# The first two of seven products summed in a PSUM bank that ScalarE fills, in a fused attention and expert kernel

## The chip, the core and the metric

The kernel runs on one core of a Trainium2 chip. TensorE multiplies matrices into PSUM, VectorE (DVE), ScalarE (ACT) and GpSimd (POOL) work on tiles of 128 partitions, and SyncE (SP) issues transfers; ScalarE issues some as well. Each engine runs its own instructions in order and waits on semaphores for the others. The metric is device time in microseconds (us): the median of the runs, here 843.47 us over three runs (843.33 to 843.47).

## The reference

What is computed is a decaying linear attention over 4 x 8 heads of 768 steps, and two expert layers on its 3072 tokens:

```python
for t in range(S):
    state = gamma[None, :, None, None] * state + np.einsum('bhd,bhe->bhde', k[:, :, t], v[:, :, t])
    y[:, :, t] = scale * np.einsum('bhd,bhde->bhe', q[:, :, t], state)
...
a = x @ w1                      # 512 -> 1024
b = x @ w2
h = a * b @ w3                  # 1024 -> 1024
x = h @ w_out                   # 1024 -> 512
...
h = np.maximum(np.maximum(x @ w1, x @ w2), x @ w3)   # 512 -> 768
return (h @ w_out).astype(np.float32)                # 768 -> 512
```

All data are float32. In the kernel every operand is split into a high and a low part of a faster float type, and a product is three matmuls: high by high, high by low, low by high.

## The kernel before, in words

The work goes in stages, with the times of the profiled execution: attention (0 to 88 us), stage B (x @ w1 and x @ w2 and their product, 88 to 320), the merging of w3 with w_out (320 to 363), its application (363 to 494), stage H (the three projections and their maximum, 494 to 752), and the output stage (752 to the end).

Stages B, H and the output stage use a scheme of seven products on a two-by-two partition of the matrices. A block (`blk`, or `n` in the output stage) is 512 columns of each half of the tokens; it goes through products `q` = 0 to 6, and each product through its parts: 4 in B (`GA`), 3 in H (`GH`), 2 in the output stage (`r`). A part is 6 matmuls of 128x512 in B and H, 9 in the output stage. The parts of a product go to one of two sets of PSUM banks, "a" or "b", which change roles from block to block. `ORDER` (L44) says which set a product uses and whether it starts afresh: product 0 starts set a; product 1 starts set b; product 2 goes on adding to a; product 3 starts b again; 4 and 6 add to a, and 5 to b.

Products are combined by evictions. In B, ScalarE copies product 0 to the tile U (L496), VectorE adds product 1 to U (L498), ScalarE copies products 2 and 3 to C and E (L500, L502), VectorE finishes E and C (L504, L506), GpSimd multiplies C by U (L507), VectorE multiplies E by the last bank (L510). H is alike (L729 to L744), with a maximum over parts: for product 1 VectorE does an add for part 0, and an add and a maximum for each of parts 1 and 2. The output stage (L787 to L803) copies product 0 to y11 and VectorE adds product 1.

Operands are made two products ahead: `op_split` (L244) lets ScalarE cast the high part (L241) and VectorE subtract the low part (L242), into one of four slots `op`. Some are differences that `op_pre` (L252) computes on VectorE, called three products ahead (`d == 3`, L472): for product 2 two instructions on 128x1024 (L255, L256, the second into the tile T), for product 3 one (L259), for product 5 one (L261).

Beside this the weights of the next stage are decoded from 64-bit numbers. `step` alternates two halves: `decode_a` (VectorE L134 for the previous piece, L140, L142 for this one) and `decode_b` (ScalarE L149, which needs L142). `decode_front` (ScalarE L117, then GpSimd L119) prepares the next piece; new pieces are fetched by transfers on ScalarE's queue (L86). The class `Spread` (L179) hands these jobs out evenly over `tick` calls, one after each part. In the first group of stage B (`g == 0`, blocks 0 to 2) the list begins with seven idle jobs (L449), over 60 ticks.

The program order of each engine is the order in which this code is written; nothing reorders it later.

## Time and profile before

| what | us |
|---|---|
| median of three runs | 843.47 |
| the profiled execution's own time | 843.5 |
| its span, first to last instruction | 841.7 |
| TensorE matmuls busy (x4720) | 830.0 (99%) |
| VectorE busy (x725) | 589.0 (70%) |
| ScalarE busy (x560) | 365.5 (43%) |
| GpSimd busy (x121) | 120.8 (14%) |
| TensorE idle for VectorE or transfers, attention left out | 2.5 in 4 waits |

The granted TensorE clock is 1.00 of full speed in every stage. Busy time of matmuls overlaps, since each is shown from its start to its modelled end: a matmul is shown 0.39 us long, though the next starts sooner. The views used are the page, the waits by engine, the timelines of each engine (instructions in order of time), and the groups by line.

### The profile page before, as it was taken

To read this page: it belongs to the slowest core of one execution; us is meant where nothing else is said; L and a number is where in the kernel's file an instruction comes from. 1 tells how busy PE (TensorE), PEld (TensorE's weight loads), DVE (VectorE), ACT (ScalarE), POOL (GpSimd) and SP (SyncE) were. 2 spreads that over 40 slices of the span, in tenths; PEclk is the share of its full clock that TensorE was granted. 3 is DMA by queue.
4 is the path that set the end of the run, shared out by engine and by line. 5 is a ranking of instruction groups with operands and counts; after the bars stand their busy time and mean duration, and the time that the engine had idled before them with its cause. 6 is when DMAs were issued, how large, how long until landed. Compare 5 with 4: busy or idle time off the path is not lost.

```text
span 841.7 us, 12200 instructions
## 1 busy us (share of the span) xinstructions
PE 830.0 (99%) x4720; PEld 694.1 (82%) x4720; DVE 589.0 (70%) x725; ACT 365.5 (43%) x560; POOL 120.8 (14%) x121
## 2 busy tenths in 40 slices
PE   8999999999999999999999999999999999999998
PEld 8889888878888888888888888887888888888886
DVE  3898978898475756753574657678657665878793
ACT  2544455354434343633555453343333334335542
POOL 3444031302031322100201000200000010000000
PEclk9999999999999999999999999999999999999999
DMA  9998367759988967462495699829998899856522
GB/s 347 408 406 337 152 283 289 288 213 369 362 324 312 340 228 263 150 218 87 147 336 213 218 410 412 334 88 382 409 361 300 318 367 357 291 239 228 209 101 75
DMA packets 54634, 235.00 MB, mean 279 GB/s; under 512 B 6320, under 2 KB 6448, under 8 KB 39344
## 3 DMA queue, kind: packets, MB, share of 16 engines
q1 hardware_dynamic: 37728, 133.46, 40.8%
q10 hardware_dynamic: 16848, 100.76, 32.5%
q8 instruction: 37, 0.61, 0.3%
q14 instruction: 21, 0.17, 0.1%
HBM read 161.85 MB, written 72.35 MB: 278 GB/s over the span
## 4 chain that ended last, share of the span: by engine, by line
PE 74%; DVE 3%; DMA 2%; issue 1%; ACT 0%; ACTq 0%; DVEq 0%
PE bank L724 9%; PE bank L725 9%; PE bank L726 9%; PE bank L492 5%; PE bank L601 5%; PE bank L603 5%; PE bank L493 5%; PE bank L602 5%; PE bank L491 5%; PE bank L783 3%; PE bank L784 3%; PE bank L782 3%; PE bank L540 2%; PE bank L542 2%; PE bank L541 2%; DMA opsp<-op 1%
## 5 line engine op out<-in xcount | busy, mean ns | idle before, releaser
L724 PE MATMUL bank<-op,w 128*128 128x512 f32 x360 | 140.1, 389 | 0.3 <-DMA op<-opsp 0.3
L725 PE MATMUL bank<-op,w 128*128 128x512 f32 x360 | 140.2, 389 | 0.2 <-DVE op L242 0.2
L726 PE MATMUL bank<-op,w 128*128 128x512 f32 x360 | 140.1, 389 | 0.0
L491 PE MATMUL bank<-op,w 128*128 128x512 f32 x336 | 130.9, 390 | 1.0 <-DVE E L510 1.0
L492 PE MATMUL bank<-op,w 128*128 128x512 f32 x336 | 130.9, 390 | 1.0 <-DVE op L242 1.0
L493 PE MATMUL bank<-op,w 128*128 128x512 f32 x336 | 130.7, 389 | 0.0
L119 POOL TENSOR_SCALAR dec<-dec 128x512 f32<-128x512 f32 x64 | 47.5, 742 | 481.6 <-ACT dec L117 457.2
L724 PEld LDWEIGHTS bank<-op,w 128*128 128x128 f32 x360 | 67.6, 188 | 14.8 <-issue 0.7
L725 PEld LDWEIGHTS bank<-op,w 128*128 128x128 f32 x360 | 67.6, 188 | 14.5 <-DVE op L242 0.6
L726 PEld LDWEIGHTS bank<-op,w 128*128 128x128 f32 x360 | 67.6, 188 | 14.1
L491 PEld LDWEIGHTS bank<-op,w 128*128 128x128 f32 x336 | 63.1, 188 | 14.7 <-ACT U L496 1.4
L492 PEld LDWEIGHTS bank<-op,w 128*128 128x128 f32 x336 | 63.1, 188 | 14.4 <-DVE op L242 1.7
L602 PE MATMUL bank<-op,w 128*128 128x512 f32 x192 | 74.7, 389 | 0.0
L601 PE MATMUL bank<-op,w 128*128 128x512 f32 x192 | 74.7, 389 | 0.0
L603 PE MATMUL bank<-op,w 128*128 128x512 f32 x192 | 74.7, 389 | 0.0
L493 PEld LDWEIGHTS bank<-op,w 128*128 128x128 f32 x336 | 63.1, 188 | 13.1
L149 ACT ACTIVATE dec<-stg 128x512 int32<-128x512 uint32 x59 | 39.6, 672 | 69.6 <-DVE stg L142 64.6
L117 ACT ACTIVATE dec<-stg 128x512 f32<-128x512 f32 x59 | 39.1, 663 | 30.3 <-DMA stg<-in_wo_dram 17.4
L140 DVE TENSOR_SCALAR dec<-dec 128x512 int32<-128x512 int32 x64 | 34.1, 533 | 23.0 <-POOL dec L119 23.0
L142 DVE SCALAR_TENSOR_TENSOR stg<-stg,dec 128x512 int32<-128x512 int32 x59 | 42.5, 720 | 5.2 <-ACT E L502 0.4
L507 POOL TENSOR_TENSOR C<-C,U 128x512 f32<-128x512 f32 x24 | 36.1, 1526 | 54.3 <-DVE C L506 54.2
L602 PEld LDWEIGHTS bank<-op,w 128*128 128x128 f32 x192 | 36.0, 188 | 7.5
(177 smaller groups left out, 1494.0 us busy)
## 6 DMA issues: line engine op xcount, KB each, us to landing
op<-opsp ACTq DMA_DIRECT2D x77, 1024.0 KB, 7.5
opsp<-op SPq DMA_DIRECT2D x25, 1024.0 KB, 5.0
ck<-in_ck_dram SPq DMA_DIRECT2D x48, 512.0 KB, 10.2
opsp<-w SPq DMA_DIRECT2D x14, 1024.0 KB, 5.9
stg<-in_w3t_dram ACTq DMA_DIRECT2D x16, 512.0 KB, 3.4
hsp<-m SPq DMA_DIRECT2D x32, 256.0 KB, 6.6
stg<-in_w_dram SPq DMA_DIRECT2D x15, 512.0 KB, 10.7
stg<-in_w_dram ACTq DMA_DIRECT2D x14, 512.0 KB, 5.1
```

The costliest lines, as they stand in the source:

```text
L119: nc.gpsimd.tensor_scalar(out=df, in0=df, scalar1=MAX_HI, scalar2=MIN_HI, op0=ALU.min, op1=ALU.max)
L142: nc.vector.scalar_tensor_tensor(out=top, in0=top, scalar=-0x40000000, in1=dec, op0=ALU.bitwise_and, op1=ALU.bitwise_or)
L149: nc.scalar.activation(out=dec, in_=low.bitcast(U32), func=ACT.Copy, scale=2.0 ** -29)
L491: nc.tensor.matmul(ps, wh, x[:, 0, k, :], start=first and k == 0, stop=False, skip_group_check=True)
L492: nc.tensor.matmul(ps, wh, x[:, 1, k, :], start=False, stop=False, skip_group_check=True)
L493: nc.tensor.matmul(ps, wl, x[:, 0, k, :], start=False, stop=k == 1, skip_group_check=True)
L601: nc.tensor.matmul(ps, wh, x[:, 0, k, :], start=kk == 0 and k == 0, stop=False)
L602: nc.tensor.matmul(ps, wh, x[:, 1, k, :], start=False, stop=False)
L603: nc.tensor.matmul(ps, wl, x[:, 0, k, :], start=False, stop=kk == 3 and k == 1)
L724: nc.tensor.matmul(ps, wh, x[:, 0, k, :], start=first and k == 0, stop=False, skip_group_check=True)
L725: nc.tensor.matmul(ps, wh, x[:, 1, k, :], start=False, stop=False, skip_group_check=True)
L726: nc.tensor.matmul(ps, wl, x[:, 0, k, :], start=False, stop=k == 1, skip_group_check=True)
```

## The change

Three things change.

First, in B (from block 1 on), in H and in the output stage, ScalarE copies product 0 not to an SBUF tile but to the bank of set b in which product 1 of the same part is about to be computed. Product 1 no longer starts that bank afresh but adds to what was copied (`seeded`; in the output stage `q != 1`). The bank then holds the sum, and ScalarE copies it out: to U in B, to m11 for part 0 in H, to y11 in the output stage. VectorE's add is gone. For parts 1 and 2 of H, VectorE takes the maximum with the bank directly, one instruction instead of two. Block 0 of B works as before.

Second, in the first group of B the two differences for product 2 of the next block are issued at product 5, behind the split of the next block's product 0, and not at product 6.

Third, the list of decode jobs in that group has four idle jobs in front instead of seven.

```diff
--- before.py
+++ after.py
@@ -446,7 +446,7 @@
             if g == 0:
                 wq += [lambda i=i, u=u: fetch_w12(i, u) for i in range(GA, KF) for u in range(2)]
                 more(3)
-                side = Spread([idle] * 7 + [step] * (4 * GA), 2 * 28 + 4)
+                side = Spread([idle] * 4 + [step] * (4 * GA), 2 * 28 + 4)
             else:
                 x_st.close()
                 m_st, m_pl = stage_pool("m")
@@ -469,11 +469,13 @@
                             t = s + d
                             if t < 7 * NB:
                                 qd = quad_b(t // 7)
-                                if d == 3:
+                                if d == 3 and t % 7 != 2:
                                     op_pre(t // 7, t % 7, qd, quiet=True)
-                                else:
+                                elif d == 2:
                                     op_split(t, op_src(t // 7, t % 7, qd))
                                     store(opsp[t // 7, t % 7], op_t[t % 4].bitcast(F32))
+                                    if q == 5:
+                                        op_pre(n + 1, 2, quad_b(n + 1), quiet=True)
                         if s < 2:
                             store(opsp[0, s], op_t[s].bitcast(F32))
                         for job in late_w.pop(s, ()):
@@ -484,15 +486,18 @@
                     which, first = ORDER[q]
                     x = op_slot(s)
                     w = wslot(q).rearrange("p h (i k n) -> p h i k n", i=GA, k=2)
+                    seeded = blk > 0 and q == 1
                     for p in range(GA):
                         ps = sets[which][p]
                         for k in range(2):
                             wh, wl = w[:, 0, p, k, :], w[:, 1, p, k, :]
-                            nc.tensor.matmul(ps, wh, x[:, 0, k, :], start=first and k == 0, stop=False, skip_group_check=True)
+                            nc.tensor.matmul(ps, wh, x[:, 0, k, :], start=first and k == 0 and not seeded, stop=False, skip_group_check=True)
                             nc.tensor.matmul(ps, wh, x[:, 1, k, :], start=False, stop=False, skip_group_check=True)
                             nc.tensor.matmul(ps, wl, x[:, 0, k, :], start=False, stop=k == 1, skip_group_check=True)
                         u, c, e = (part(nm, p) for nm in "UCE")
                         if q == 0:
+                            nc.scalar.copy(out=sets["b"][p] if blk else u, in_=ps)
+                        elif seeded:
                             nc.scalar.copy(out=u, in_=ps)
                         elif q == 1:
                             nc.vector.tensor_tensor(out=u, in0=u, in1=ps, op=ALU.add)
@@ -717,27 +722,29 @@
                     which, first = ORDER[q]
                     x = quads4(gen_t[s - held] if held <= s < held + len(gen_t) else op_t[s % 4])
                     w = wslot(q, 256 * GH).rearrange("p h (i k n) -> p h i k n", i=GH, k=2)
+                    seeded = q == 1
                     for p in range(GH):
                         ps = sets[which][p]
                         for k in range(2):
                             wh, wl = w[:, 0, p, k, :], w[:, 1, p, k, :]
-                            nc.tensor.matmul(ps, wh, x[:, 0, k, :], start=first and k == 0, stop=False, skip_group_check=True)
+                            nc.tensor.matmul(ps, wh, x[:, 0, k, :], start=first and k == 0 and not seeded, stop=False, skip_group_check=True)
                             nc.tensor.matmul(ps, wh, x[:, 1, k, :], start=False, stop=False, skip_group_check=True)
                             nc.tensor.matmul(ps, wl, x[:, 0, k, :], start=False, stop=k == 1, skip_group_check=True)
                         u, c, e = (part(nm, p) for nm in "UCE")
                         if q == 0:
-                            nc.scalar.copy(out=u, in_=ps)
+                            nc.scalar.copy(out=sets["b"][p], in_=ps)
                         elif q == 2:
                             nc.scalar.copy(out=c, in_=ps)
                         elif q == 3:
                             nc.scalar.copy(out=e, in_=ps)
-                        elif q == 6:
+                        elif q in (1, 6):
+                            m = m12 if q == 6 else m11
                             if p:
-                                nc.vector.tensor_tensor(out=m12, in0=m12, in1=ps, op=ALU.max)
+                                nc.vector.tensor_tensor(out=m, in0=m, in1=ps, op=ALU.max)
                             else:
-                                nc.scalar.copy(out=m12, in_=ps)
+                                nc.scalar.copy(out=m, in_=ps)
                         else:
-                            m, v, (x0, x1), op = {1: (m11, u, (u, ps), ALU.add), 4: (m22, e, (ps, e), ALU.subtract),
+                            m, v, (x0, x1), op = {4: (m22, e, (ps, e), ALU.subtract),
                                                   5: (m21, c, (c, ps), ALU.subtract)}[q]
                             nc.vector.tensor_tensor(out=v if p else m, in0=x0, in1=x1, op=op)
                             if p:
@@ -779,14 +786,14 @@
                 ps = o_sets[n % 2][which][r]
                 o = slice(r * P, (r + 1) * P)
                 for k in range(3):
-                    nc.tensor.matmul(ps, wh[:, k, o], xh[:, k], start=first and k == 0, stop=False, skip_group_check=True)
+                    nc.tensor.matmul(ps, wh[:, k, o], xh[:, k], start=first and k == 0 and q != 1, stop=False, skip_group_check=True)
                     nc.tensor.matmul(ps, wh[:, k, o], xl[:, k], start=False, stop=False, skip_group_check=True)
                     nc.tensor.matmul(ps, wl[:, k, o], xh[:, k], start=False, stop=k == 2, skip_group_check=True)
                 y11, y12, y21, y22 = y_t[4 * r:4 * r + 4]
                 if q == 0:
+                    nc.scalar.copy(out=o_sets[n % 2]["b"][r], in_=ps)
+                elif q == 1:
                     nc.scalar.copy(out=y11, in_=ps)
-                elif q == 1:
-                    nc.vector.tensor_tensor(out=y11, in0=y11, in1=ps, op=ALU.add)
                     store(outv[r, 0, :, cols], y11, 0)
                 elif q == 2:
                     nc.scalar.copy(out=y21, in_=ps)
```

How the instructions now stand is told by their order, here at three places. Numbers at the end of a tile's name tell copies of a tile apart: bank_1094 to bank_1097 are set a of block 1 in B, and bank_1090 to bank_1093 its set b. Line numbers from L447 on differ between the two kernels.

ScalarE in stage B, around product 0 of block 1, before:

```order
L117 ACTIVATE dec_63<-stg_62 128x512
L241 CAST op_1103<-xr_94 128x1024
L149 ACTIVATE dec_63<-stg_62 128x512
L117 ACTIVATE dec_64<-stg_60 128x512
L241 CAST op_73<-xr_94 128x1024
L149 ACTIVATE dec_64<-stg_60 128x512
L117 ACTIVATE dec_63<-stg_61 128x512
L86 DMA stg_62<-in_w_dram 128x512
L241 CAST op_1101<-T 128x1024
L496 COPY U<-bank_1094 128x512
L496 COPY U<-bank_1095 128x512
L496 COPY U<-bank_1096 128x512
```

And with the change:

```order
L241 CAST op_1103<-xr_94 128x1024
L149 ACTIVATE dec_64<-stg_60 128x512
L117 ACTIVATE dec_63<-stg_61 128x512
L86 DMA stg_62<-in_w_dram 128x512
L241 CAST op_73<-xr_94 128x1024
L149 ACTIVATE dec_63<-stg_61 128x512
L117 ACTIVATE dec_64<-stg_62 128x512
L86 DMA stg_60<-in_w_dram 128x512
L241 CAST op_1101<-T 128x1024
L499 COPY bank_1090<-bank_1094 128x512
L499 COPY bank_1091<-bank_1095 128x512
L499 COPY bank_1092<-bank_1096 128x512
```

The last L149 and L117 ahead of the cast of T now belong to the next piece of weights (stg_61 and stg_62, where it was stg_60 and stg_61), so one decode step more lies ahead of the cast in all, and the copies behind it go to banks instead of U.

VectorE in stage B, from the evictions of C in block 0 to the first eviction of E, before:

```order
L506 TENSOR_TENSOR C<-C,bank_1094 128x512
L506 TENSOR_TENSOR C<-C,bank_1095 128x512
L506 TENSOR_TENSOR C<-C,bank_1096 128x512
L506 TENSOR_TENSOR C<-C,bank_1097 128x512
L134 ISA wraw<-stg_62,dec_63 128x2x512
L140 TENSOR_SCALAR dec_64<-dec_64 128x512
L142 SCALAR_TENSOR_TENSOR stg_60<-stg_60,dec_64 128x512
L255 TENSOR_TENSOR xr_94<-xr_94 128x2x512
L256 TENSOR_TENSOR T<-xr_94 128x1024
L242 TENSOR_TENSOR op_73<-xr_94,op_73 128x1024
L510 TENSOR_TENSOR E<-E,bank_1090 128x512
```

And with the change:

```order
L242 TENSOR_TENSOR op_1103<-xr_94,op_1103 128x1024
L255 TENSOR_TENSOR xr_94<-xr_94 128x2x512
L256 TENSOR_TENSOR T<-xr_94 128x1024
L511 TENSOR_TENSOR C<-C,bank_1094 128x512
L511 TENSOR_TENSOR C<-C,bank_1095 128x512
L511 TENSOR_TENSOR C<-C,bank_1096 128x512
L511 TENSOR_TENSOR C<-C,bank_1097 128x512
L242 TENSOR_TENSOR op_73<-xr_94,op_73 128x1024
L515 TENSOR_TENSOR E<-E,bank_1090 128x512
L134 ISA wraw<-stg_60,dec_64 128x2x512
L140 TENSOR_SCALAR dec_63<-dec_63 128x512
L142 SCALAR_TENSOR_TENSOR stg_61<-stg_61,dec_63 128x512
```

L255 and L256 stand ahead of the evictions of C, the decode triple that stood behind them is gone from here, and the next triple (dec_63, stg_61) now stands behind the first eviction of E; ScalarE's L149 above on stg_61 needs its last instruction.

ScalarE at the start of stage H, before:

```order
L204 CAST w_68<-wraw_h 128x768
L204 CAST w_69<-s_t 128x768
L204 CAST w_70<-wraw_h 128x768
L204 CAST w_71<-wraw_h 128x768
L580 DMA op_1103<-opsp 128x2048
L729 COPY U<-bank_1094 128x512
L729 COPY U<-bank_1095 128x512
```

And with the change:

```order
L204 CAST w_68<-wraw_h 128x768
L204 CAST w_69<-s_t 128x768
L204 CAST w_70<-wraw_h 128x768
L204 CAST w_71<-wraw_h 128x768
L585 DMA op_1103<-opsp 128x2048
L735 COPY bank_1097<-bank_1094 128x512
L735 COPY bank_1090<-bank_1095 128x512
```

The weight casts ahead are the same (w_68 to w_71); the copies behind them now fill banks.

## Rows read from the trace of the kernel before

**Rows 1.** Page, part 1: busy us, share of the span, instructions.
```profile
PE 830.0 (99%) x4720; PEld 694.1 (82%) x4720; DVE 589.0 (70%) x725; ACT 365.5 (43%) x560; POOL 120.8 (14%) x121
```

**Rows 2.** TensorE timeline at its four waits: start us, us, operation, idle before.
```profile
171.41 0.47 PE L491 MATMUL bank<-op,w 128*128 128x512 f32 x1 [1.02 <-DVE E L510]
...
189.30 0.50 PE L492 MATMUL bank<-op,w 128*128 128x512 f32 x1 [1.03 <-DVE op L242]
...
567.86 0.50 PE L725 MATMUL bank<-op,w 128*128 128x512 f32 x1 [0.18 <-DVE op L242]
...
584.59 0.47 PE L724 MATMUL bank<-op,w 128*128 128x512 f32 x1 [0.30 <-DMA op<-opsp]
```

**Rows 3.** TensorE timeline where products 0 and 1 of a block meet.
```profile
127.84 0.39 PE L493 MATMUL bank<-op,w 128*128 128x512 f32 x1
...
132.15 0.39 PE L491 MATMUL bank<-op,w 128*128 128x512 f32 x1
...
289.85 0.39 PE L491 MATMUL bank<-op,w 128*128 128x512 f32 x1
...
497.93 0.39 PE L724 MATMUL bank<-op,w 128*128 128x512 f32 x1
...
756.07 0.39 PE L782 MATMUL bank<-w,wo 128*128 128x512 f32 x1
```

**Rows 4.** ScalarE timeline before block 1 of stage B.
```profile
111.18 1.08 ACT L241 CAST op<-xr 128x1024 fp32r<-128x1024 f32 x1
...
126.83 0.68 ACT L149 ACTIVATE dec<-stg 128x512 int32<-128x512 uint32 x1 [7.04 <-DVE stg L142]
...
127.40 0.66 ACT L117 ACTIVATE dec<-stg 128x512 f32<-128x512 f32 x1
129.27 1.05 ACT L241 CAST op<-T 128x1024 fp32r<-128x1024 f32 x1 [1.21 <-issue]
130.22 1.55 ACT L496 COPY U<-bank 128x512 f32<-128x512 f32 x3
```

**Rows 5.** VectorE timeline before block 1 of stage B.
```profile
112.30 1.22 DVE L242 TENSOR_TENSOR op<-xr,op 128x1024 fp32r<-128x1024 f32 x1 [1.67 <-ACT op L241]
113.44 1.22 DVE L205 TENSOR_TENSOR w<-wraw,w 128x1024 fp32r<-128x1024 f32 x1
...
119.22 1.88 DVE L506 TENSOR_TENSOR C<-C,bank 128x512 f32<-128x512 f32 x3
...
122.07 1.59 DVE L134 CUSTOM_DVE_ANT_0 wraw<-stg,dec 128x1024 uint16<-128x1024 uint16 x1
...
125.19 1.61 DVE L142 SCALAR_TENSOR_TENSOR stg<-stg,dec 128x512 int32<-128x512 int32 x1
...
135.32 0.68 DVE L134 CUSTOM_DVE_ANT_0 wraw<-stg,dec 128x1024 uint16<-128x1024 uint16 x1
...
136.38 0.69 DVE L142 SCALAR_TENSOR_TENSOR stg<-stg,dec 128x512 int32<-128x512 int32 x1
```

**Rows 6.** GpSimd timeline in the same stretch.
```profile
121.82 4.42 POOL L507 TENSOR_TENSOR C<-C,U 128x512 f32<-128x512 f32 x3
```

**Rows 7.** ScalarE timeline at the first block of stage H.
```profile
496.62 0.83 ACT L204 CAST w<-s_t 128x768 fp32r<-128x768 f32 x1 [1.25 <-DMA opsp<-w]
...
498.83 1.55 ACT L729 COPY U<-bank 128x512 f32<-128x512 f32 x3
```

**Rows 8.** ScalarE timeline at the first block of the output stage.
```profile
755.60 1.48 ACT L666 CAST w<-m 128x1536 fp32r<-128x1536 f32 x1 [5.54 <-DVE m L654]
756.98 1.07 ACT L787 COPY stg<-bank 128x512 f32<-128x512 f32 x2
```

**Rows 9.** ScalarE timeline at block 5 of stage B.
```profile
288.88 0.67 ACT L117 ACTIVATE dec<-stg 128x512 f32<-128x512 f32 x1 [2.33 <-DMA stg<-in_w3t_dram]
...
289.46 0.57 ACT L496 COPY U<-bank 128x512 f32<-128x512 f32 x1
```

**Rows 10.** Groups by line, ScalarE: busy us, mean ns, idle before, releasers.
```profile
L729 ACT COPY U<-bank 128x512 f32<-128x512 f32 x27 | 15.5, 587 | 24.0 <-PE bank L726 22.1 <-DVE m L736 1.7
```

## The prediction

> **What bounds the kernel now.** I read the page's first part: TensorE's matmuls are busy 830.0 us of the 841.7 us span [rows 1]. Nothing on another engine matters unless TensorE waits for it, so next came TensorE's waits, and then its timeline at each of them. Outside the attention stage at the start, which the change does not touch, it waits four times [rows 2]: 1.02 and 1.03 us in the first group of stage B, both for VectorE, and 0.18 and 0.30 us in stage H. The third is again for VectorE; the fourth is for an operand load whose store was issued behind the late VectorE result of the third. Between waits a matmul starts every 0.227 us (19 starts from 127.84 to 132.15 [rows 3]), while each is shown 0.39 us long. An idle gap therefore costs its length plus 0.16 us: 1.18 + 1.19 + 0.34 + 0.46 = 3.2 us. That is all a relieved VectorE could return.
>
> **What the change does to each engine.** From the order: VectorE loses 53 instructions (20 adds in B, 27 in H, 6 in the output stage), ScalarE gains 35 copies, TensorE keeps the same matmuls. Some 36 us of VectorE work go (53 of about 0.68 us), but they are worth only the 3.2 us above.
>
> The price is a new wait. Product 0's copy now writes the bank into which product 1 accumulates, so TensorE cannot start a part of product 1 before the copy of that part is done. Before, that copy had until product 2 reused its source bank. Now it has from the end of its part's matmuls until the same part comes round: 3.9 us in B (132.15 minus 127.84 minus 0.39 [rows 3]), 2 parts of 1.36 us minus the 0.16 us drain in H (2.6 us), 9 matmuls minus drain in the output stage (1.9 us). The copy itself takes about 0.59 us. ScalarE works in order, so whatever stands before the copy counts. The 27 copies in H were idle 24.0 us before them in all, 22.1 of it waiting for TensorE itself [rows 10]: mostly they are on time and their cover is about 2 us. So I looked for the blocks where the old copy ended after product 1 had started. A copy of TensorE's own bank into another bank does not stand in this trace; I take the 0.59 us of the copy to SBUF, bounded by nothing and by twice that, since the bank is read the same way; either bound moves each stall below by 0.6 us.
>
> The Trainium skill ("ScalarE: Activation LUTs", Step-by-step) says that ScalarE writes PSUM faster than SBUF; no run here shows it yet, and by it each new stall would be a few tenths of a microsecond shorter.
>
> **Block 0 of H.** ScalarE's last weight casts wait until 496.62 for a store that still reads their slot, and the copies start at 498.83 [rows 7]. The first ended at 498.83 + 0.59 = 499.42; product 1 started at 497.93 [rows 3]. The change alters nothing ahead of these copies, so TensorE now waits 1.5 us. The store's landing may come 0.8 us earlier or later: 0.7 to 2.3.
>
> **Block 0 of the output stage.** The cast ahead of the copy waits for VectorE's L654, starts at 755.60, and the copies start at 756.98 [rows 8]; the first ends at 757.57, where product 1 started at 756.07. VectorE's queue up to L654 holds no instruction that the change removes and hangs from TensorE's products 4 and 5 of the last H block, so it does not move against TensorE: 1.5 us (1.3 to 1.7).
>
> **Block 5 of B.** Part 2's copy stood behind a decode step that waited for weights (288.88) and ended at 289.46 + 0.57 = 290.03, its matmul starting at 289.85 [rows 3, 9]: 0.2 us, and up to 1.2 if those weights land a microsecond later. Nothing else in the second group is late.
>
> **Block 1 of B**, the largest and least certain term. Before, ScalarE did a decode step at 126.83 and 127.40, the cast of T at 129.27, and the copies from 130.22 [rows 4]; the first ended at 130.8, before the 132.15 of product 1. But decoding now begins three steps ahead, and the order shows one more decode step (L149, L117) in front of this cast and these copies; L149 waits for VectorE's L142, which stands behind the first E eviction. So I lay VectorE's queue end to end. The split of op_1102 started at 112.30 [rows 5], after its cast at 111.18 [rows 4]; three ScalarE decode instructions now go ahead of that cast (0.57 us each, from 126.83 to 127.40) and one of them waits some 0.5 us for VectorE, so it starts about 114.6. Up to that L142 follow six 128x1024 operations at 1.14 us (112.30 to 113.44), nine evictions at 0.60, and two decode triples of 1.75 us (135.32 to 136.38 + 0.69): 6.84 + 5.4 + 3.5 = 15.7, so it ends at 130.3 if nothing disturbs it. When GpSimd multiplies C by U, the triple took 4.73 us instead (122.07 to 125.19 + 1.61 [rows 5, 6]), which gives 133.3. GpSimd's four products take 1.47 us each (4.42 over 3) and one clamp 0.6; they start with the first C eviction, about 125.1, and end at 131.6, while the triple starts at 128.6. So two of its three are stretched: 132.4. Then 0.57 + 0.57 + 0.95 + 0.59 us on ScalarE [rows 4] bring the first seed to 135.1 against 132.15: TensorE waits 2.9 us, bounds 0.9 and 3.9.
> By the Trainium skill ("SBUF — State Buffer", Who interferes with whom) VectorE and GpSimd share an SBUF port pair under an exclusive lock, and the loser blocks for the whole instruction. The triple's stretch from 1.75 to 4.73 us agrees; taken for all three instructions the stall is the 3.9 us, and the forecast 1.0 us later.
>
> **What goes in return.** With TensorE some 3 us later at block 1, VectorE 0.6 us per removed add ahead, and the two op_pre differences one product earlier, the E evictions and the split that ended the waits at 171.41 and 189.30 are done in time: minus 2.4 us. Moving op_pre earlier delays the C evictions behind it by some 2.3 us; their bank is needed a whole product later, which hides it. The decode's earlier fetches only start sooner into free buffers. In H three adds per block fewer, and a TensorE 1.5 us later, take away the two waits of [rows 2]: minus 0.8; should VectorE's work stay tied to the later product 1, they remain (0). In the output stage six adds less meet no wait. What is late next is then ScalarE, at the four places above.
>
> **Sum** on the profiled execution (span 841.7, time 843.5 against a median of 843.47, so one basis serves for both): 2.9 - 2.4 + 0.2 + 1.5 - 0.8 + 1.5 = +2.9 us, that is 846.4.
>
> **Rivals.**
> A. The cover at block 1 nearly holds: GpSimd's products miss the triple and the stall is 0.9. For it: evictions from PSUM are not stretched in the trace, and the C evictions could run earlier. Against: GpSimd starts right behind them. Sum +0.9: 844.4, no change that can be told.
> B. Faster: the relieved VectorE brings ScalarE forward so far that no seed is late except in the output stage, whose queue loses nothing. All four waits go and 1.5 comes: 843.5 - 3.2 + 1.5 = 841.8, and 840.3 if that one goes too. It decides where block 1's L142 ends before 129.5 and H's store lands before 495. Against it stand the order (a decode step more ahead of the seeds) and 496.62.
> C. The lateness carries on: in block 2 a decode step stands between seeds 1 and 2 as well, waiting for an L142 behind three E evictions. If VectorE has not caught up there, TensorE waits a second time, 1.5 us or more, and H's waits stay (0.8): 843.5 + 2.9 + 1.5 + 0.8 = 848.7.
>
> **How the numbers follow.** The forecast 0.55 (own range 845.0 to 848.0), A 0.25, B 0.08, C 0.12. The range 843.0 to 849.0 takes in A and C, the bounds of block 1 and H, and leaves out B. A measurement here tells 0.2% (1.7 us) from nothing: faster means under 841.8, slower over 845.2. Nearly all of the forecast and C are slower, 0.64; A and its edges are the same, 0.28; B is 0.08.
>
> **What would show it.** In the changed profile TensorE's waits should name ScalarE's copies into a bank (L499, L735, L794): about 3 us at the second product of block 1 in B, about 1.5 us at the first H block and the first output block. The waits near 171, 189, 568 and 585 should be gone. No wait at block 1 makes A or B right; a second one near 176 makes C right. The forecast is wrong at its root if TensorE's waits on ScalarE are under 2 us in all.

## The result, and the profile after

The changed kernel takes 851.07 us in the median of five runs (849.71 to 853.2), the kernel before 843.34 on the same chip (843.05 to 843.47): a ratio of 1.0092, interval 1.0076 to 1.0108. It is slower by 7.7 us. The forecast was 846.4 with a range of 843.0 to 849.0: the sign was right, the size was less than half of what came, and the time lies outside the range.

The profiled execution has a span of 849.3 us, 7.6 more than [rows 1]. The page of the changed kernel, part 1 (busy us, share of the span, instructions), and the line of part 2 with the clock that TensorE was granted, in 40 slices:

```profile
PE 832.0 (98%) x4720; PEld 695.7 (82%) x4720; DVE 556.5 (66%) x672; ACT 384.8 (45%) x595; POOL 116.0 (14%) x121
...
PEclk9999998999999999999999999999999999999999
```

VectorE lost the 53 instructions and 32.5 us of busy time (36 were worked out); the end shows none of it. New is the 8 in the clock's line (in tenths, a 9 is 90% or more): on the page of the kernel before, every slice of that line is a 9.

TensorE's waits (us in total, times, longest):

```profile
PE bank L494 <- ACT bank L499: 4.4, 2, 3.8
...
PE bank L789 <- ACT bank L794: 1.7, 1, 1.7
PE bank L730 <- ACT bank L735: 1.6, 1, 1.6
```

Behind attention every wait now names a copy of ScalarE into a bank; the four of [rows 2] are gone. TensorE's timeline at these four places (start us, us, operation, idle before and its releaser):

```profile
132.03 0.39 PE L496 MATMUL bank<-op,w 128*128 128x512 f32 x1
136.25 0.79 PE L494 MATMUL bank<-op,w 128*128 128x512 f32 x1 [3.84 <-ACT bank L499]
136.84 0.63 PE L495 MATMUL bank<-op,w 128*128 128x512 f32 x1
137.27 0.63 PE L496 MATMUL bank<-op,w 128*128 128x512 f32 x1
...
141.49 0.40 PE L494 MATMUL bank<-op,w 128*128 128x512 f32 x1
...
255.09 0.50 PE L494 MATMUL bank<-op,w 128*128 128x512 f32 x1 [0.52 <-ACT bank L499]
...
504.55 0.50 PE L730 MATMUL bank<-op,w 128*128 128x512 f32 x1 [1.65 <-ACT bank L735]
...
763.66 0.50 PE L789 MATMUL bank<-w,wo 128*128 128x512 f32 x1 [1.73 <-ACT bank L794]
```

Where products 0 and 1 of block 1 meet, matmul starts are 4.23 us apart (132.03 to 136.25) instead of 0.227: 4.0 us lost. The next starts are not 0.227 apart but 0.427 (136.84, 137.27 and so on): each matmul takes twice as long. That lasts for twelve starts, until 141.49. From 136.25 to 141.49 the twelve take 5.24 us where 12 x 0.227 = 2.72 would do: 2.5 us more. The windows name the cause (length, busy us of the five engines, then the granted clock, the DMA share, GB/s):

```profile
136.00:141.50 5.50, 5.25 (x13) 4.13 (x14) 5.47 (x7) 3.22 (x6) 0.00 (x0) 0.51 0.99 395
141.50:500.00 358.50, 357.99 (x1579) 296.12 (x1578) 216.99 (x272) 172.25 (x259) 60.66 (x56) 1.00 0.70 259
```

The granted clock is 0.51 just behind the wait, which is the lower level of 1.2 GHz, and 1.00 (2.4 GHz) after it. It fell within the 3.84 us in which TensorE stood idle: in the window from 134.60 to 136.20, in which no matmul starts, it is 0.50 already.

Taken from the gaps between starts, all of the difference is accounted for. A matmul that restarts is followed by one late start of about 0.34 us, which is counted with its wait:

| place | forecast us | measured us |
|---|---|---|
| block 1 of B, wait for the first copy | +2.9 | +4.0 |
| block 1 of B, matmuls at half clock behind it | none | +2.5 |
| the two waits in B [rows 2] | -2.4 | -2.6 |
| second group of B | +0.2 (block 5) | +0.8 (block 4) |
| block 0 of H | +1.5 | +1.9 |
| the two waits in H [rows 2] | -0.8 | -1.0 |
| block 0 of the output stage | +1.5 | +2.0 |
| sum | +2.9 | +7.6 |

Why ScalarE is late at block 1 stands in its timeline and in VectorE's, which answer to [rows 4] and [rows 5]. ScalarE:

```profile
133.57 0.67 ACT L149 ACTIVATE dec<-stg 128x512 int32<-128x512 uint32 x1 [10.84 <-DVE stg L142]
...
134.14 0.65 ACT L117 ACTIVATE dec<-stg 128x512 f32<-128x512 f32 x1
134.70 1.03 ACT L241 CAST op<-T 128x1024 fp32r<-128x1024 f32 x1
135.63 1.54 ACT L499 COPY bank<-bank 128x512 f32<-128x512 f32 x3
```

VectorE:

```profile
127.08 2.00 DVE L242 TENSOR_TENSOR op<-xr,op 128x1024 fp32r<-128x1024 f32 x1
129.01 0.67 DVE L515 TENSOR_TENSOR E<-E,bank 128x512 f32<-128x512 f32 x1
129.61 1.77 DVE L134 CUSTOM_DVE_ANT_0 wraw<-stg,dec 128x1024 uint16<-128x1024 uint16 x1
131.30 1.51 DVE L140 TENSOR_SCALAR dec<-dec 128x512 int32<-128x512 int32 x1
132.84 0.69 DVE L142 SCALAR_TENSOR_TENSOR stg<-stg,dec 128x512 int32<-128x512 int32 x1
```

And GpSimd, beside it [rows 6]:

```profile
125.45 2.55 POOL L512 TENSOR_TENSOR C<-C,U 128x512 f32<-128x512 f32 x2 [11.03 <-DVE C L511]
127.95 1.61 POOL L119 TENSOR_SCALAR dec<-dec 128x512 f32<-128x512 f32 x1
129.53 3.00 POOL L512 TENSOR_TENSOR C<-C,U 128x512 f32<-128x512 f32 x2
```

ScalarE stood still for 10.84 us, waiting for L142, and did the decode step and the cast before the first copy, which took 0.57 us and ended at 136.20; it was due at 132.26 (132.03 + 0.227). GpSimd's five instructions run from 125.45 to 132.5 (129.53 + 3.00), and in that time three of VectorE's that read only SBUF are long: 2.00, 1.77 and 1.51 us, while the eviction from PSUM between them takes its usual 0.6.

### The profile page after: what moved, and what is told of

It reads as the page before. It is cut to its first block, busy times and chain, and to the rows that moved or that the text cites. A ratio compares the mean times of both kernels' runs of the same rounds, so it can differ in the third digit from the quotient of the medians.

```text
span 849.3 us, 12189 instructions
## 1 busy us (share of the span) xinstructions
PE 832.0 (98%) x4720; PEld 695.7 (82%) x4720; DVE 556.5 (66%) x672; ACT 384.8 (45%) x595; POOL 116.0 (14%) x121
## 4 chain that ended last, share of the span: by engine, by line
PE 81%; DMA 8%; issue 5%; DVE 4%; ACT 1%; POOL 0%; SPq 0%; ACTq 0%; POOLq 0%; DVEq 0%
PE bank L730 10%; PE bank L732 10%; PE bank L731 10%; PE bank L494 7%; PE bank L495 7%; PE bank L496 7%; DMA ck<-in_ck_dram 7%; PE bank L608 5%; PE bank L607 5%; PE bank L606 5%; PE bank L789 3%; PE bank L791 3%; PE bank L790 3%; PE bank L547 2%; PE bank L546 2%
## 5 line engine op out<-in xcount | busy, mean ns | idle before, releaser
L119 POOL TENSOR_SCALAR dec<-dec 128x512 f32<-128x512 f32 x64 | 43.5, 680 | 484.5 <-ACT dec L117 465.4
L149 ACT ACTIVATE dec<-stg 128x512 int32<-128x512 uint32 x59 | 39.6, 671 | 64.5 <-DVE stg L142 59.6
L140 DVE TENSOR_SCALAR dec<-dec 128x512 int32<-128x512 int32 x64 | 35.0, 547 | 35.4 <-POOL dec L119 35.4
L117 ACT ACTIVATE dec<-stg 128x512 f32<-128x512 f32 x59 | 38.9, 659 | 14.0 <-DMA stg<-in_w3t_dram 7.5
L142 DVE SCALAR_TENSOR_TENSOR stg<-stg,dec 128x512 int32<-128x512 int32 x59 | 41.8, 708 | 4.3
```

The costliest lines, as they stand in the source:

```text
L119: nc.gpsimd.tensor_scalar(out=df, in0=df, scalar1=MAX_HI, scalar2=MIN_HI, op0=ALU.min, op1=ALU.max)
L142: nc.vector.scalar_tensor_tensor(out=top, in0=top, scalar=-0x40000000, in1=dec, op0=ALU.bitwise_and, op1=ALU.bitwise_or)
L149: nc.scalar.activation(out=dec, in_=low.bitcast(U32), func=ACT.Copy, scale=2.0 ** -29)
```

## The experiments

The theory: the copies into banks make TensorE wait for whatever stands ahead of them on ScalarE, at block 1 for the decode step that the third part of the change puts there; the wait brings the half clock with it. Two rivals are tried beside it: that the second part (the earlier differences) is to blame by delaying VectorE, and that the copies cost the time by themselves. All ratios are to the kernel before, measured beside each run; a 95% interval stands behind each. The lost time of a wait is the gap between starts less 0.227.

### The change without its third part

```diff
-                side = Spread([idle] * 4 + [step] * (4 * GA), 2 * 28 + 4)
+                side = Spread([idle] * 7 + [step] * (4 * GA), 2 * 28 + 4)
```

> The changed kernel with seven idle jobs ahead of the decode list again, all else as changed. Theory W (ScalarE's decode step, waiting for a VectorE triple that the earlier decode put behind the first eviction of E, holds up the copies into the bank at block 1; the 4.0 us wait is what lets the clock fall): the gating triple is back ahead of that eviction, the wait at block 1 goes to under 0.5 us, the granted clock is 1.00 throughout, and the waits of 0.9 us at block 4 of B, 1.9 in H and 2.0 in the output stage stay: 843.3 - 3.6 + 4.8 + about 0.3 in block 2 = 844.8 (843.8 to 846). Rival P (the earlier differences put GpSimd's products on top of the triple and are the cause): the wait stays near 4 us and the time at 849 to 852. Rival K (copies from bank to bank are slow or disturb TensorE by themselves): 849 to 852 too.

Measured: 844.94 us (842.42 to 847.77), 1.0020 (1.0007 to 1.0033), before 843.25. TensorE's waits outside attention:

```profile
PE bank L789 <- ACT bank L794: 1.7, 1, 1.7
...
PE bank L730 <- ACT bank L735: 0.9, 1, 0.9
...
PE bank L494 <- ACT bank L499: 0.5, 1, 0.5
```

Its window around block 1, with the granted clock third from the end:

```profile
125.00:145.00 20.00, 20.00 (x90) 16.58 (x89) 17.32 (x20) 12.00 (x20) 7.00 (x6) 1.00 0.86 314
```

There is no wait at block 1 and no half clock: 20.00 us of 20.00 are busy at 1.00. The three late copies elsewhere remain; in H 1.2 us are lost, late start included, where 1.9 were expected. Some 6 of the 7.7 us hang on the three idle jobs. The execution in the trace took 843.62 us, 1.3 less than the median.

### The change without its second part

```diff
-                                if d == 3 and t % 7 != 2:
+                                if d == 3:
                                     op_pre(t // 7, t % 7, qd, quiet=True)
...
-                                    if q == 5:
-                                        op_pre(n + 1, 2, quad_b(n + 1), quiet=True)
```

> The changed kernel with the differences for product 2 at product 6 again, the decode still three steps earlier. Theory W: the same VectorE work stands ahead of the gating triple, so block 1 still waits 3 to 4.5 us, the clock falls again for some microseconds, and the time is 849 to 852. Rival P: the wait at block 1 falls below 1 us, the clock stays at 1.00, 844 to 846. Rival K: 849 to 852.

Measured: 850.89 us (849.38 to 851.81), 1.0089 (1.0071 to 1.0106). At block 1 starts are 3.80 apart, so 3.6 us are lost where the whole change loses 4.0, and the half clock follows for eight starts:

```profile
135.65 0.50 PE L492 MATMUL bank<-op,w 128*128 128x512 f32 x1 [3.41 <-ACT bank L497]
```

So the earlier differences are not to blame. That the total is as long too is partly chance: H loses only 0.3 us here, the output stage 2.3 us and a second stretch of half clock (last section). VectorE's timeline shows that the queue has only changed places under GpSimd's work:

```profile
124.39 2.00 DVE L255 TENSOR_TENSOR xr<-xr 128x1024 f32<-128x1024 f32 x1
...
127.86 2.31 DVE L242 TENSOR_TENSOR op<-xr,op 128x1024 fp32r<-128x1024 f32 x1
...
132.24 0.69 DVE L142 SCALAR_TENSOR_TENSOR stg<-stg,dec 128x512 int32<-128x512 int32 x1
```

Now L255, L256 (1.52) and the split are long, and the triple is shorter (L134 1.18, L140 0.41). L142 starts at 132.24 instead of 132.84, only 0.6 us earlier: taking work out from under GpSimd's products puts other work there.

### Parts two and three without the copies into banks

The diff to the kernel before is parts two and three of the change, as shown ahead of the prediction.

> The kernel before with the earlier differences and the earlier decode, but no copy into a bank anywhere: VectorE adds product 1 as before. Theories W and K: no wait on ScalarE; TensorE's two waits for VectorE in B become shorter since VectorE fills earlier idle time, those in H stay: 841.8 to 843.4. Rival P (the order of VectorE's work alone delays TensorE): over 845, with a wait at block 1.

Measured: 841.61 us (841.47 to 842.97), 0.9978 (0.9969 to 0.9987): faster than the kernel before. The two waits of [rows 2] in B are gone, with one short one in their place; those in H stay. TensorE:

```profile
134.28 0.51 PE L493 MATMUL bank<-op,w 128*128 128x512 f32 x1 [0.42 <-DVE E L512]
```

That wait, for an eviction of E behind the decode triple, loses 0.6 us. VectorE's split, L134 and L140 are as long here as in the changed kernel (2.01, 1.76 and 1.51), and ScalarE's copies of product 0 are as late:

```profile
135.73 2.02 ACT L498 COPY U<-bank 128x512 f32<-128x512 f32 x4
```

But these go to SBUF, and TensorE does not wait for them. The same decode three steps ahead that costs 6 us with the copies into banks costs at most those 0.6 us without them.

### The copies into banks alone

The diff to the kernel before is the first part of the change.

> The kernel before with the copies into the bank alone: decode and differences where they were. Theory W: in block 1 the copies end 1.3 us ahead of product 1 as in the trace before, no wait there, clock 1.00; up to 1 us in block 2, 0.9 in block 4, 1.9 and 2.0 at the first blocks of H and the output stage, against 3.6 saved: 845.0 (844 to 846.5). Rival P: the same. Rival K (each copy from bank to bank costs by itself): 849 or more, with waits on ScalarE at most blocks.

Measured: 845.33 us (842.90 to 850.15), 1.0032 (1.0015 to 1.0048), granted clock 1.00 in the profiled run. From the gaps between starts, 1.77 us are lost at the first block of H, 1.88 at that of the output stage, and 0.1 to 0.5 us at each of four places in B. So the first part alone is worth +2.1 us, parts two and three alone -1.6, and together they make +7.7: some 7 us are neither's own but come from their meeting. The copies do not cost that by themselves.

### The change with one decode step behind the copies of block 1

The order on VectorE and GpSimd is that of the changed kernel. Only ScalarE's L149 and L117 (with their fetch) move from ahead of the cast and the four copies to behind them.

```diff
+        def held_ticks(blk, q, p):
+            return (blk, q) == (1, 0) or (blk, q, p) == (0, 6, GA - 1)
...
-                        side.tick()
+                        if not held_ticks(blk, q, p):
+                            side.tick()
+                    if blk == 1 and q == 0:
+                        for _ in range(GA + 1):
+                            side.tick()
```

> The changed kernel with one decode step (L149 and L117 on ScalarE, the clamp on GpSimd) issued behind the four copies of block 1 instead of ahead of them; VectorE's order is that of the changed kernel, instruction for instruction. Theory W (the copies are late because ScalarE stands at that L149): the first copy follows TensorE at once; parts 1 to 3 still wait for the E evictions behind the triple (about 134.1 in the changed kernel's trace, against 133.5 needed), so some 1.2 us of wait remain of 4.0, and the clock does not fall for long: 851.1 - 2.8 - 2.6 = 845.7 (844.5 to 848). Rival V (VectorE itself, which holds the bank until its evictions are done, is the cause): the wait stays at 4 us, 849 to 852.

Measured: 846.20 us (844.70 to 847.33), 1.0028 (1.0018 to 1.0038), before 843.56. ScalarE's copies:

```profile
129.77 0.57 ACT L502 COPY bank<-bank 128x512 f32<-128x512 f32 x1 [3.86 <-PE bank L499]
134.20 1.77 ACT L502 COPY bank<-bank 128x512 f32<-128x512 f32 x3 [3.86 <-DVE E L518]
```

The matmul that waits, on TensorE:

```profile
134.83 0.50 PE L497 MATMUL bank<-op,w 128*128 128x512 f32 x1 [1.05 <-ACT bank L502]
```

The first copy is in time, and of the 4.0 us 1.2 are left, without half clock. What is left is another dependence of these copies: the bank that the second one fills is still to be read by VectorE's second eviction of E of the block before (L518), which stands behind the decode triple. In the kernel before, only the matmul waited for that eviction; now a copy of 0.57 us stands between. The waits in H and the output stage grew to 2.2 and 2.4 us in this run (from 1.8 and 1.9, late start left out), so the time does not fall by all that block 1 gave back.

### The change without GpSimd's product of C and U in block 0

```diff
-                            nc.gpsimd.tensor_tensor(out=c, in0=c, in1=u, op=ALU.mult)
+                            if blk:
+                                nc.gpsimd.tensor_tensor(out=c, in0=c, in1=u, op=ALU.mult)
```

> The changed kernel without GpSimd's four multiplications of C by U in block 0 of each group of stage B (left out: that factor of those blocks' result). Nothing else moves. If the shared use of SBUF by VectorE and GpSimd made the gating triple late, the split, L134, L140 and L142 ahead of block 1 take 1.14, 0.60, 0.46 and 0.69 us again, L142 ends near 130.6 instead of 133.5, TensorE waits about 1.1 us instead of 4.0, and the clock does not fall there: 851.1 - 2.9 - 2.6 = 845.6 (844.5 to 847). Rival Q (the triple is late by VectorE's own queue, the stretch only fills time in which it would wait anyway): the wait stays over 3 us and the time at 849 to 852.

Measured: 846.80 us (845.53 to 847.63), 1.0038 (1.0025 to 1.0052), before 843.43. VectorE:

```profile
127.56 1.22 DVE L242 TENSOR_TENSOR op<-xr,op 128x1024 fp32r<-128x1024 f32 x1
...
129.29 0.68 DVE L134 CUSTOM_DVE_ANT_0 wraw<-stg,dec 128x1024 uint16<-128x1024 uint16 x1
129.89 0.42 DVE L140 TENSOR_SCALAR dec<-dec 128x512 int32<-128x512 int32 x1
130.34 0.69 DVE L142 SCALAR_TENSOR_TENSOR stg<-stg,dec 128x512 int32<-128x512 int32 x1
```

TensorE at block 1:

```profile
133.77 0.50 PE L494 MATMUL bank<-op,w 128*128 128x512 f32 x1 [1.20 <-ACT bank L499]
```

Split, L134 and L140 have their short lengths (1.22, 0.68, 0.42). The lost time at block 1 falls from 4.0 to 1.4 us and the half clock does not come. So of the 4.0 us 2.6 are GpSimd's products stretching VectorE's queue, and 1.4 are the order itself, near the 0.9 that the prediction gave for an undisturbed queue. Some 0.3 us of the 1.4 are not the order's: VectorE came to the split 0.5 us later than in the changed kernel (127.56 against 127.08), TensorE to the end of product 0 only 0.15 later. Taken from the three lengths, the stretch in the changed kernel is 0.78 + 1.09 + 1.09 = 3.0 us.

### What makes copies late moved behind them, with the copies kept

This joins what the runs before pointed to: seven idle jobs again; in B the decode ticks of product 0 come after its four copies; in H the last three weight casts, and in the output stage the split for its third product, are issued behind the first copies.

```diff
-                side = Spread([idle] * 4 + [step] * (4 * GA), 2 * 28 + 4)
+                side = Spread([idle] * 7 + [step] * (4 * GA), 2 * 28 + 4)
...
-                        side.tick()
+                        if q or not blk:
+                            side.tick()
+                    if q == 0 and blk:
+                        for _ in range(GA):
+                            side.tick()
...
-        for q in range(4, 7):
-            wgen(q)
+        wgen_first = wgen
...
+                    if blk == 0 and q == 0:
+                        for z in range(4, 7):
+                            wgen_first(z)
...
-            o_split(s + 2)
+            if s:
+                o_split(s + 2)
...
+            if s == 0:
+                o_split(s + 2)
```

> The changed kernel with what stood ahead of the late copies moved behind them: seven idle jobs, so that the gating triple is ahead of block 1's E evictions; in B the decode ticks of product 0 after its four copies; the last three weight casts of stage H after product 0 of its first block; in the output stage the cast for product 2 after the first copies. Theory W: no wait on ScalarE above 0.3 us, and none on VectorE: 843.3 - 3.6 = 839.8 (839.2 to 841). Rival D (work moved behind the copies comes late itself): waits for operands or weights take their place, 842 to 846.

Measured: 840.94 us (839.70 to 842.67), 0.9972 (0.9963 to 0.9982). All three of TensorE's waits in its trace lie in attention; the longer two:

```profile
PE pair L317 <- DMA ck<-in_ck_dram: 3.2, 5, 0.8
PE abank L400 <- POOL st L383: 1.3, 1, 1.3
```

The same kernel was measured a second time, side by side with the version that follows it:

> The kernel of the run e5_moved, in the same call as its version without copies into a bank: 840.9 (839.7 to 842), no wait of TensorE on ScalarE above 0.3 us.

Measured: 840.45 us (839.69 to 840.85), 0.9963 (0.9951 to 0.9976), before 843.43. In this trace one wait of 0.4 us is left in the output stage, for VectorE.

And with the same moves but no copy into a bank at all (product 0 goes to SBUF and VectorE adds product 1, as in the kernel before):

> The kernel of the run e5_moved without any copy into a bank: VectorE adds product 1 again, everything that was moved stays moved. If the copies into the bank still bring something once nothing stands ahead of them, VectorE's waits come back (about 0.6 to 2 us in B, 0.9 in H) and this is 1 to 2.5 us slower than that kernel in the same call: 841.5 to 843. If only the moved work mattered, the two agree within 0.5 us.

Measured, beside that second measurement: 841.77 us (841.41 to 842.79), 0.9982 (0.9973 to 0.9991). A wait for VectorE's split is back in B:

```profile
187.71 0.50 PE L495 MATMUL bank<-op,w 128*128 128x512 f32 x1 [0.67 <-DVE op L242]
```

So the relief of VectorE is worth 841.77 - 840.45 = 1.3 us once nothing stands ahead of the copies (the two ranges do not overlap). The other 1.7 of the 3.0 us that the moved version gains come without any copy into a bank. The version with the moves beats both kernels, by 0.3 to 0.4% and, from medians taken at different times, by some 1.2%.

### Waits of several lengths in stage H

The kernel of the last section, with 6, 8, 10 and 12 more copies of ScalarE to U ahead of the first copy in blocks 1, 3, 5 and 7 of H; their results are overwritten.

```diff
                         if q == 0:
+                            if p == 0:
+                                for z in range({1: 6, 3: 8, 5: 10, 7: 12}.get(blk, 0)):
+                                    nc.scalar.copy(out=part("U", z % 4), in_=ps)
                             nc.scalar.copy(out=sets["b"][p], in_=ps)
```

> The kernel of the run e5_moved with 6, 8, 10 and 12 extra ScalarE copies (0.48 us apart, results unused) ahead of the first copy into a bank in blocks 1, 3, 5 and 7 of stage H. They should make TensorE wait about 1.0, 2.0, 2.9 and 3.9 us. If the half clock belongs to a long wait, the granted clock stays at 1.00 behind the first and falls behind the longest, where some ten matmuls start 0.43 us apart: sum about 10.3 us of waits and restarts and 2 to 6 us of clock, 852 to 856. If the clock fell in the changed kernel for a reason of stage B alone, it stays at 1.00 behind all four: 850.

Measured: 858.32 us in a single run, above the range expected. TensorE's timeline at the four restarts:

```profile
525.30 0.50 PE L733 MATMUL bank<-op,w 128*128 128x512 f32 x1 [0.89 <-ACT bank L741]
...
586.22 0.80 PE L733 MATMUL bank<-op,w 128*128 128x512 f32 x1 [3.50 <-ACT bank L741]
...
649.40 0.50 PE L733 MATMUL bank<-op,w 128*128 128x512 f32 x1 [2.85 <-ACT bank L741]
...
712.26 0.79 PE L733 MATMUL bank<-op,w 128*128 128x512 f32 x1 [3.83 <-ACT bank L741]
```

The windows behind them:

```profile
525.00:534.00 9.00, 8.70 (x38) 7.23 (x39) 5.48 (x6) 5.68 (x11) 2.98 (x2) 1.00 1.01 377
586.00:594.00 8.00, 7.78 (x21) 6.15 (x22) 1.15 (x2) 1.73 (x4) 0.00 (x0) 0.60 0.93 383
649.00:657.00 8.00, 7.59 (x26) 6.13 (x27) 4.08 (x6) 3.70 (x7) 0.00 (x0) 0.79 0.44 155
712.00:720.00 8.00, 7.74 (x28) 6.29 (x29) 2.50 (x5) 3.43 (x7) 0.61 (x1) 0.79 0.48 152
```

Behind 0.89 us idle the clock stays at 1.00. Behind 3.50, 2.85 and 3.83 it is 0.60, 0.79 and 0.79 in the mean of the window, with stretches of matmuls 0.427 apart. The sizes of the waits were not those I had forecast from the number of copies (3.7 us lost in block 3 and 3.0 in block 5, where 2.0 and 2.9 were expected), nor was the total. What the run shows is that long waits bring the half clock in another stage and with another cause of the wait; it does not give the number of slow matmuls for a length, since behind 3.83 us there are 7 slow starts and behind 3.50 us fourteen.

## Why the prediction was right in sign and wrong in size

**The mechanism and the places** were right. TensorE waits on ScalarE's copies at block 1 of B, at the first block of H and at the first block of the output stage, and the four waits of [rows 2] went. Taking the third part away brought 851.07 down to 844.94; taking the copies away brought it to 841.61. A copy from bank to bank takes 0.57 us, at the price taken for it (0.59), and not at either bound. The rule cited beside it (the Trainium skill, "ScalarE: Activation LUTs", Step-by-step) has the right sign, but is worth 0.02 us here (0.57 against the 587 ns of [rows 10]), not the few tenths, for which no row stood.

**The step that failed: an idle gap costs its length.** The prediction read from [rows 2] and [rows 3] that a gap costs its length plus 0.16 us. That held, to 0.1 us each, for the four waits of about a microsecond and less which the trace of before has, and I carried it over to a wait of 3 us. Behind the 4.0 us wait the granted clock was 0.51 and twelve matmuls cost 2.5 us more. No term and no rival had this, and the range had no room for it beside the other misses (846.4 + 2.5 alone is 848.9). Half of the miss of 4.7 us is this one. The full clock throughout the trace of before was a fact about a kernel that never waits long, and not one about the changed kernel.

**The term mis-sized: block 1.** 2.9 us were forecast within 0.9 and 3.9; it was 4.0. The way was right (L142 behind a stretched queue, then decode step, cast and copy: 0.57 + 0.57 + 0.93 + 0.57 us from 133.57 on), but GpSimd's work took a longer stretch of the queue than I laid under it. I had it stretch two instructions of the triple, by 2 us in all. It stretched the split ahead of the triple as well (2.00 instead of 1.22), and L134 and L140 by 1.1 each: 3.0 us in all, which is 0.9 of the 1.1 that the term lacks. Without GpSimd's products the wait is 1.4 us, so by that run the contention is 2.6 of the 4.0. By the Trainium skill ("SBUF — State Buffer", Who interferes with whom) one of the two engines blocks for the whole instruction of the other. The run without the products shows that they are what makes the three long, but not that a block lasts a whole instruction. The sum by that rule, 3.9 us, was nearer than mine, partly by luck: it stretched the whole triple, and the split was stretched in place of L142.

**The smaller terms** were each right in place and a little short: 1.9 instead of 1.5 in H, where the cast that waits for a store began about 0.3 us later against TensorE than in [rows 7], and 2.0 instead of 1.5 in the output stage, where the cast behind VectorE began 0.35 us later than in [rows 8]; a late start of 0.1 us is in each. In the second group of B the late copy moved from block 5 to block 4, where ScalarE, by its timeline, stood 2.10 us for weights and 1.36 us for VectorE's L140 ahead of it. These three make 1.5 us of the miss, and the relief was 0.4 larger than forecast, because the restart's second late start was not counted.

**The rivals.** A (the cover nearly holds) needed VectorE's queue undisturbed; the run without GpSimd's products is nearest to it, with 1.4 us and 846.80 where A had 0.9 and 844.4. C (lateness carries on to block 2) did not come: starts are 0.227 apart behind 141.5. B (faster) hung on what stands ahead of the copies; it did not come, but the kernel with the moves, which is another kernel, is what it described: no copy late, 840.45 to 840.94.

**Left open.** Which of two waits of like length brings the half clock is not settled by these runs (below). The kernels with late copies scatter more from run to run (842.4 to 847.8 for the change without its third part and 842.9 to 850.2 for the copies alone, with mean granted clocks of 0.996 to 1.000, against 842.8 to 845.0 for the kernel before beside them); the traces show one execution each, so it is not shown where the others lose the time.

## What to carry to other kernels

When a result that nobody waited for becomes the input of the bounding engine's next instruction, take the time at which it is due and lay end to end, on the engine that makes it, everything that stands ahead; then move that work behind it before judging the saving. Price a forecast wait of some microseconds on TensorE with the matmuls behind it at half rate too, even where the trace of before shows full clock throughout. Where VectorE and GpSimd meet, count every VectorE instruction that reads only SBUF in GpSimd's time as stretched, as in these traces, not only those of the queue's end.

## What the runs showed of the hardware

The half clock does not follow the length of the wait alone. In the run without the second part, the output stage waited 2.15 us, and the clock fell about half a microsecond after the restart:

```profile
761.01 0.50 PE L787 MATMUL bank<-w,wo 128*128 128x512 f32 x1 [2.15 <-ACT bank L792]
```

Its windows:

```profile
761.00:762.00 1.00, 0.99 (x3) 0.81 (x4) 1.00 (x2) 0.44 (x1) 0.00 (x0) 0.76 1.01 311
762.00:765.00 3.00, 3.00 (x9) 2.31 (x7) 3.00 (x3) 1.63 (x2) 0.00 (x0) 0.51 0.91 303
```

In the run with the decode step behind, the same place waited slightly longer, and the starts behind it are 0.23 apart, without a fall:

```profile
758.52 0.50 PE L796 MATMUL bank<-w,wo 128*128 128x512 f32 x1 [2.25 <-ACT bank L801]
```

In H the same run waited 1.99 us, without a fall either. So in these traces no half clock followed on idle stretches of up to 1.73 us; of the three of 1.99, 2.15 and 2.25 us the middle one had it, and so had all five of 2.85 to 3.84 us. What else decides is not shown, and no length is to be taken from it. The Trainium skill ("TensorE: Matmul & The Clock Gate", Part 1) says that the number of slow matmuls differs between runs of one kernel; no run here shows that, since no kernel with a slow stretch has a second trace. What the traces show is 12 slow starts behind 3.84 us idle in the changed kernel and 7 behind 3.83 us in the last experiment, which are different kernels.

Filling a bank from ScalarE and adding matmuls to it costs TensorE nothing by itself: with every copy in time, B's matmuls start 0.227 us apart through the change of products (the kernel with the moves).
